# Windowed attention with sinks and a rational feed-forward layer: one sum of the gate made by an adding transfer in SBUF, all window masks on VectorE, and another program order

## The chip, the cores and the metric

The kernel runs on one core of one Trainium2 chip. A core has TensorE (matmuls, called PE in the profile), VectorE (DVE), ScalarE (ACT), GpSimd (POOL) and SyncE (SP), a memory on the core (SBUF), accumulators that matmuls write (PSUM), and 16 DMA engines that all queues share. The metric is the device time of one execution in microseconds, as the median of several. Lower is better.

## What is computed

The reference, cut to what matters:

```python
# q, k, v: (4 batches, 8 heads, 768 positions, 64), float32
scores = (1 / 8) * q @ k.T
keep = (pos_k < 4) | ((pos_q - pos_k >= 0) & (pos_q - pos_k < 128))
a = softmax(where(keep, scores, -1e9))
x = (a @ v) laid out as (3072 tokens, 512)
h = x @ w_in                                  # (3072, 2048)
P = a0 + a1*h + a2*h*h + a3*h*h*h
Q = 1 + |b0|*|h| + |b1|*h*h
out = (P / (Q + 1e-6)) @ w_out                # (3072, 512)
```

Each query sees 4 sink positions and a window of 128. Behind the attention comes a layer whose gate is a rational function, P/Q, of every element of h.

## The kernel before

**Steps.** The 3072 tokens are cut into 12 steps of 256 tokens, three to a batch. Every step goes through the same pieces: load q, k and v (POOL queue, which casts from float32 to bf16 on the way), turn k and q so that the head dimension lies on the partitions (by TensorE in the first steps, by transposing DMAs of the SP queue later), scores of each of the four head pairs (L466), exponentials (ACT, L489), the window mask, the attention product (L518), its normalisation (DVE, L542), the turned x (L568 to L598), the product with `w_in` in four slices (`gemm1`, L605), the gate, and the product with `w_out` in two halves for each of two rows of 128 tokens (`gemm2`, L669).

**The gate.** For one step h is a tile of 128 x 4096 in bf16. The gate takes it through these steps, in one piece for steps 1 to 10, in three for step 0 and in four for step 11 (`cuts`, L935):

- `copy_in` (ACT, L614): h out of PSUM, in four slices.
- `square` (L620): half of it on ACT, half on DVE; `SQ_ACT` (L120) can name another number of quarters for ACT by step.
- `magnitude` and `denominator` (DVE, L628, L634): |h| + h squared, after a scaling of x that makes the coefficients 1.
- `log_den` and `recip_den` (ACT, L653, L657): 1/Q as exp(-ln Q).
- `even` (DVE, L637): a0 + a2 h², into the tile `num`.
- `odd` and `odd_h` (DVE, L643, L647): (a1 + a3 h²) h, in place in the tile `sq`.
- `numerator` (DVE, L650): `num` + `sq`.
- `gate` (DVE, L661): `num` times 1/Q, into the tile `g`, which `gemm2` reads.

There are two buffers each of `hb`, `sq`, `den` and `g`, and one of `num`. So `even` of a step waits for `gate` of the step before, and `gate` waits for `gemm2` of two steps before.

**The masks.** Scores are computed in blocks of 64 keys by 192 queries, whose two outer thirds are cut by the triangles of the window. In the steps that `PE_MASK` (L119) names, TensorE adds a large negative number to the forbidden places by further matmuls into the same PSUM (L479 to L486). In the others DVE multiplies the exponentials with a tile of ones and zeros, `edge` (L498), one instruction for two head pairs.

**The order.** Nothing is scheduled at build time. Each piece of work has a number in the table `work` (from L697 on); the list `ORDER` (L18) is the order in which the pieces are issued, and with it the order of every engine's instructions. A negative entry is so many matmuls on a dummy tile (`spin`, L437). The figures in `piece(...)` (length, rank, load) do not act at run time. Semaphores between engines follow from the tiles. An engine runs its instructions in the order given, so a waiting instruction holds up whatever stands behind it on its engine. A transfer issued from POOL waits in the same way: for the data it reads, and for the transfer eight before it, whose semaphore it takes over.

Of the kernel before, what the change touches and what calls it, by code (L numbers as in the profile page):

```python
# [9 lines left out]
FP32 = mybir.dt.float32  # L10
BF16 = mybir.dt.bfloat16
# [7 lines left out]
    0, 2, 163, 164, 162, 154, 165, 167, 3, 166, 152, 11, 8, 151, 5, 10, 153, 12, 14, 13, 6, 15, 9,  # L19
    21, 143, 174, 1, 169, 190, -47, 191, 155, 199, 202, 196, 179, -30, 197, 172, 194, 170, 208, 195,  # L20
    160, 201, 161, 209, 157, 171, 206, 4, 7, 20, 22, 17, 145, 26, 25, 16, 24, 18, 19, 23, 192, 207,
    210, -13, 193, 200, 204, 180, 156, 212, 198, 214, 173, 181, 211, 213, 203, 205, 216, 250, 252,
    -15, 243, 217, 251, 244, -7, 218, 270, 246, 253, 219, 245, 178, 158, 271, 255, 262, 248, 247,
    249, 215, 260, 276, 159, 263, 168, 177, 261, 254, 258, 277, 256, 259, 257, 264, 278, 267, 279,
    268, 272, 265, 266, 274, 273, 220, 275, 221, 269, 579, 280, 296, 577, 281, 580, 149, 147, 184,
    30, 36, 27, 37, 38, 297, 596, 595, 282, 283, 302, 286, 583, 578, 597, 175, 586, 598, 287, 284,
    585, 587, 285, 590, 600, 601, 581, 288, 599, 584, 303, 289, 582, 317, 290, 306, 291, 293, 298,
    222, 307, 304, 292, 299, 223, 294, 323, 295, 35, 33, 32, 148, 34, 31, 39, 29, 28, 144, 47, 46,
    182, 146, 43, 48, 51, 50, 49, 185, 40, 42, 41, 150, 188, 45, 187, 186, 44, 183, 189, 224, 588,
    225, 305, 591, 602, 605, 603, 606, 604, 607, 176, 324, 592, 309, 629, 630, 625, 300, 352, 351,  # L30
    226, 314, 608, 627, 301, 626, 227, 589, 628, 308, 610, 593, 315, 312, 611, 313, 594, 609, 612,
    623, 310, 320, 332, 228, 229, 353, 624, 333, 321, 615, 311, 613, 345, 318, 319, 330, 322, 654,
    331, 632, 328, 329, 655, 652, 334, 325, 653, 335, 326, 337, 633, 614, 631, 634, 637, 327, 638,
    639, 650, 616, 342, 635, 617, 651, 316, 656, 343, 336, 354, 340, 341, 619, 338, 348, 363, 640,
    620, 339, 657, 636, 364, 346, 349, 347, 350, 361, 59, 52, 58, 61, 54, 53, 60, 62, 63, 380, 71,
    64, 57, 73, 56, 72, 55, 379, 230, 381, 355, 362, 659, 677, 359, 683, 360, 357, 678, 681, 621,
    356, 358, 682, 684, 344, 622, 618, 66, 69, 68, 67, 65, 70, 407, 74, 75, 85, 660, 641, 658, 366,
    661, 382, 365, 664, 642, 367, 679, 389, 687, 368, 665, 369, 643, 370, 666, 662, 390, 680, 385,
    371, 372, 386, 644, 374, 408, 376, 409, 77, 83, 76, 97, 373, 391, 375, 377, 392, 646, 663, 378,
    387, 647, 708, 383, 706, 388, 384, 709, 686, 648, 707, 667, 685, 394, 410, 393, 668, 395, 704,  # L40
    396, 688, 397, 710, 398, 691, 399, 669, 400, 692, 693, 401, 79, 231, 87, 84, 82, 86, 96, 233,
    81, 78, 80, 645, 437, 232, 418, 649, 402, 404, 436, 465, 464, 234, 235, 438, 466, 705, 689, 670,
    419, 711, 671, 420, 411, 673, 421, 416, 713, 412, 417, 403, 405, 406, 735, 414, 736, 415, 690,
    714, 694, 413, 712, 422, 423, 439, 428, 429, 731, 426, 715, 427, 467, 732, 695, 674, 737, 424,
    442, 733, 675, 716, 443, 700, 718, 425, 719, 430, 448, 701, 734, 738, 449, 720, 440, 446, 109,
    493, 676, 433, 702, 447, 441, 740, 696, 444, 431, 94, 89, 90, 108, 93, 92, 95, 98, 107, 100, 88,
    102, 91, 99, 110, 103, 236, 672, 703, 492, 494, 445, 432, 434, 435, 762, 763, 741, 739, 451,
    721, 456, 764, 450, 457, 717, 742, 454, 455, 758, 474, 452, 461, 697, 765, 759, 475, 121, 105,
    101, 106, 111, 104, 239, 113, 118, 115, 119, 112, 114, 120, 117, 116, 470, 722, 453, 745, 495,
    746, 768, 747, 698, 471, 743, 458, 760, 723, 472, 724, 468, 473, 761, 476, 459, 699, 237, 238,  # L50
    522, 521, 477, 767, 766, 478, 479, 469, 460, 462, 463, 789, 785, 725, 523, 744, 790, 482, 769,
    483, 727, 480, 505, 728, 506, 786, 503, 729, 504, 770, 748, 481, 749, 484, 485, 772, 524, 773,
    508, 791, 750, 501, 496, 787, 497, 792, 502, 788, 498, 513, 487, 726, 499, 486, 500, 751, 774,
    514, 507, 793, 795, 511, 512, 133, 126, 122, 489, 240, 131, 124, 123, 241, 127, 134, 550, 242,
    488, 490, 491, 816, 509, 533, 771, 775, 510, 817, 752, 534, 794, 818, 531, 532, 814, 529, 525,
    754, 819, 815, 530, 776, 796, 132, 128, 125, 135, 130, 137, 142, 139, 136, 140, 138, 141, 129,
    526, 797, 812, 799, 536, 800, 822, 516, 518, 730, 549, 755, 756, 813, 757, 753, 517, 519, 527,
    528, 520, 839, 541, 551, 801, 552, 542, 535, 820, 802, 777, 843, 537, 778, 561, 840, 798, 821,
    538, 803, 539, 515, 845, 540, 844, 562, 559, 779, 846, 560, 826, 823, 841, 842, 849, 827, 564,
    828, 847, 553, 557, 780, 546, 544, 545, 547, 781, 554, 558, 824, 548, 555, 782, 783, 556, 866,  # L60
    569, 804, 868, 848, 867, 825, 543, 563, 570, 805, 829, 850, 565, 566, 806, 869, 870, 808, 567,
    830, 853, 568, 809, 872, 854, 807, 784, 572, 574, 573, 575, 871, 851, 810, 811, 873, 875, 852,
    855, 831, 876, 874, 856, 877, 857, 576, 832, 895, 893, 833, 896, 894, 878, 835, 899, 836, 897,
    837, 900, 879, 858, 859, 834, 860, 838, 861, 862, 863, 880, 881, 901, 882, 911, 883, 931, 884,
    902, 898, 912, 922, 903, 916, 906, 913, 907, 921, 864, 885, 886, 904, 932, 914, 865, 887, 889,
    908, 923, 933, 926, 917, 909, 927, 905, 910, 947, 890, 941, 918, 928, 919, 936, 915, 934, 924,
    920, 925, 935, 891, 929, 937, 930, 938, 939, 948, 942, 949, 943, 571, 940, 950, 944, 951, 945,
    946, 892, 888, 952
# [4 lines left out]
def kernel(  # L73
# [45 lines left out]
    PE_MASK = (0, 1, 2, 3, 6, 9)  # L119
    SQ_ACT = {}  # L120
# [62 lines left out]


    k_bf, v_bd, q_bf = {}, {}, {}

    stage_a = m_sb.tile([P, MW], BF16, tag="sq", name="stage_a").bitcast(FP32)
    raw_k = stage_a[:, 0:NTS * H * D]
    stage_b = m_sb.tile([P, MW], BF16, tag="num", name="stage_b", bufs=1).bitcast(FP32)
    raw_q = stage_b[:, 0:NQ0 * H * D]  # L190
    stage_s = const_pool.tile([NS * H, D], FP32, name="stage_s")
    early = m_sb.tile([P, MW], BF16, tag="g", name="early").rearrange("p (t c) -> p t c", c=H * D)
    early_k = early[:, 0:NTS, :]
    early_q = early[:, NTS:NTS + NQ0, :]

# [868 lines left out]
```

The softmax here doesn't subtract the row's maximum and nothing guards it: scores larger than these inputs give would overflow.

## Time and profile before

| | |
|---|---|
| median of 5 runs | 255.29 us (254.15 to 257.38) |
| the profiled execution | 255.35 us, of which the profile's span is 253.6 us |
| mean granted TensorE clock | 0.993 of full speed |
| TensorE, busy | 238.2 us, 94% of the span |
| DVE, busy | 227.2 us, 90% |
| ACT, busy | 223.5 us, 88% |
| POOL, busy (issuing transfers) | 119.8 us, 47% |
| DMA moved | 27.11 MB, 107 GB/s on average |
| transfers of the POOL queue | 75568 packets, 13.00 MB |

1.75 us of the profiled execution lie outside the span. Times inside the profile count from the span's start. A row of a group gives line, engine, operation, output and inputs, the shapes and the count, then the sum of busy time, the mean of one instruction, and the idle time of the engine before them. Instructions of an engine overlap at their ends by some 0.08 us, so the distance from start to start is a little shorter than the mean: 2.20 us for a DVE operation on 128 x 4096 in bf16, whose mean is 2.28 us.

### The profile page before, as it was taken

The page shows a single profiled execution, that of the slowest core. Times are in us where ns is not written, and L with a number is a line of the kernel's source. Part 1 is how long each engine was busy: PE and PEld are TensorE (multiplying, and loading weights), DVE is VectorE, ACT ScalarE, POOL GpSimd, SP SyncE. Part 2 cuts the span into 40 slices and gives each one's busy share as a digit, 9 for nine tenths or more (in the row PEclk, how much of TensorE's full clock was granted, in tenths as well). Part 3 has the DMA queues.
Part 4 walks back from the last instruction along what each step waited for, and adds up shares of the span by engine and source line. Part 5 has one row for each costly group of instructions (what it writes and reads, how often), then busy time and mean ns, then how long its engine had stood idle before and what let it go on. Part 6 is the DMA issues. An engine that isn't in the chain of part 4 may idle for free.

```text
span 253.6 us, 5192 instructions
## 1 busy us (share of the span) xinstructions
PE 238.2 (94%) x2100; PEld 177.3 (70%) x2100; DVE 227.2 (90%) x294; ACT 223.5 (88%) x209; POOL 119.8 (47%) x170
## 2 busy tenths in 40 slices
PE   8585999999999999999999999999999999998894
PEld 7584898879667769687587676786776775763341
DVE  5238299999999999999999999999999999999991
ACT  6464699989999988989998999999999998999970
POOL 7987869698995266099905609840000000000000
PEclk9889999999999999999999999999999999999999
DMA  5999999999999989999995959994205023111103
GB/s 140 156 141 154 169 135 157 179 117 137 89 139 133 97 88 184 133 124 141 134 141 64 153 58 120 138 77 106 84 0 85 0 85 83 41 44 41 41 26 141
DMA packets 107056, 27.11 MB, mean 107 GB/s; under 512 B 97816, under 2 KB 103960, under 8 KB 107032
## 3 DMA queue, kind: packets, MB, share of 16 engines
q0 software_dynamic: 75568, 13.00, 71.2%
q1 hardware_dynamic: 29936, 12.72, 26.1%
q10 hardware_dynamic: 1528, 1.06, 1.5%
q8 instruction: 16, 0.26, 0.5%
q14 instruction: 8, 0.07, 0.1%
HBM read 27.30 MB, written 6.29 MB: 132 GB/s over the span
## 4 chain that ended last, share of the span: by engine, by line
PE 54%; DVE 25%; ACT 10%; DMA 6%; issue 3%
PE ps_out L678 21%; PE ps_h L610 19%; PE ps_o L538 6%; DVE num L651 3%; PE ps_s L476 3%; DMA stage_b<-in_q_dram 3%; DVE sq L648 2%; DVE num L640 2%; DVE kT L427 2%; ACT hb L617 2%; DVE x_n L562 2%; DVE sq L644 2%; DVE g L664 2%; DMA stage_s<-in_v_dram 2%; DVE den L635 2%
## 5 line engine op out<-in xcount | busy, mean ns | idle before, releaser
L610 PE MATMUL ps_h<-xblk,w_in_sb 128*128 128x256 bf16 x768 | 91.2, 273 | 0.3
L678 PE MATMUL ps_out<-w_out_sb,g 128*128 128x512 bf16 x368 | 86.4, 379 | 2.1 <-ACT o_t L687 2.1
L610 PEld LDWEIGHTS <-w_in_sb 128*128 128x128 bf16 x768 | 74.1, 98 | 11.2 <-issue 0.8
L241 POOL DMA_DIRECT2D v_bd<-in_v_dram x96 | 65.8, 704 | 28.0 <-PE ps_o L538 21.7
L678 PEld LDWEIGHTS <-g 128*128 128x128 bf16 x384 | 37.0, 98 | 40.2 <-issue 2.9
L617 ACT ACTIVATE hb<-ps_h 128x1024 bf16<-128x1024 f32 x48 | 48.8, 1036 | 4.8 <-PE ps_h L610 4.1
L654 ACT ACTIVATE lnq<-den,one_eps,qsc 128x4096 f32<-128x4096 bf16 (+2 forms) x17 | 47.5, 2803 | 0.5 <-DVE den L635 0.5
L494 ACT ACTIVATE e<-ps_s 128x768 bf16<-128x768 f32 x48 | 39.4, 822 | 6.8 <-PE ps_s L484 3.5
L659 ACT ACTIVATE den<-lnq 128x4096 bf16<-128x4096 f32 (+2 forms) x17 | 44.4, 2624 | 0.1
L538 PE MATMUL ps_o<-v_bd,e 128*128 128x130 bf16 x352 | 28.8, 220 | 3.8 <-DVE x_n L562 1.3
L538 PEld LDWEIGHTS <-e 128*128 128x128 bf16 x352 | 23.9, 97 | 8.4 <-DVE x_n L562 3.3
L233 POOL DMA_DIRECT2D k_bf<-in_k_dram x22 | 22.0, 1002 | 14.7 <-DMA kT_flat<-k_bf 12.1
L635 DVE TENSOR_TENSOR den<-den,sq 128x4096 bf16<-128x4096 bf16 (+2 forms) x17 | 28.1, 1658 | 0.7 <-ACT sq L624 0.5
L664 DVE TENSOR_TENSOR g<-num,den 128x4096 bf16<-128x4096 bf16 (+2 forms) x17 | 28.2, 1658 | 0.5 <-ACT den L659 0.3
L648 DVE TENSOR_TENSOR sq<-sq,hb 128x4096 bf16<-128x4096 bf16 (+2 forms) x17 | 28.1, 1659 | 0.1
L651 DVE TENSOR_TENSOR num<-num,sq 128x4096 bf16<-128x4096 bf16 (+2 forms) x17 | 28.1, 1656 | 0.0
L476 PE MATMUL ps_s<-qT,kT 128*128 128x192 bf16 x192 | 26.3, 246 | 0.5 <-ACT e L494 0.5
L624 ACT ACTIVATE sq<-hb 128x2048 bf16<-128x2048 bf16 (+1 forms) x15 | 24.3, 1630 | 0.0
L225 POOL DMA_DIRECT2D q_bf<-in_q_dram x21 | 19.1, 914 | 4.8 <-DMA w_out_sb<-in_moe_w_out_dram 2.0
L476 PEld LDWEIGHTS <-kT 128*128 128x128 bf16 x192 | 16.7, 98 | 4.7 <-issue 1.0
L562 DVE SCALAR_TENSOR_TENSOR x_n<-ps_o,ratio,rec 128x384 bf16<-128x384 f32 (+1 forms) x33 | 18.9, 573 | 1.2
L644 DVE TENSOR_SCALAR sq<-sq,acoef 128x4096 bf16<-128x4096 bf16 (+2 forms) x17 | 18.5, 1088 | 0.1
(88 smaller groups left out, 240.7 us busy)
## 6 DMA issues: line engine op xcount, KB each, us to landing
out_dram<-o_t SPq DMA_DIRECT2D x22, 256.0 KB, 2.5
v_bd<-in_v_dram POOLq DMA_DIRECT2D x96, 32.0 KB, 4.8
k_bf<-in_k_dram POOLq DMA_DIRECT2D x22, 128.0 KB, 5.4
q_bf<-in_q_dram POOLq DMA_DIRECT2D x21, 128.0 KB, 5.4
w_in_sb<-in_moe_w_in_dram POOLq DMA_DIRECT2D x4, 512.0 KB, 7.5
w_out_sb<-in_moe_w_out_dram POOLq DMA_DIRECT2D x4, 512.0 KB, 7.0
stage_b<-in_q_dram ACTq DMA_DIRECT2D x2, 384.0 KB, 7.3
stage_a<-in_k_dram SPq DMA_DIRECT2D x2, 256.0 KB, 4.2
```

Source lines behind the costliest of these rows:

```text
L241: nc.gpsimd.dma_start(out=v_bd[s][e * 64:(e + 1) * 64, i, :, e, 0:D], in_=v[b, h, g * TS:(g + 1) * TS, :].rearrange("(j p) d -> p j d", p=64))
L476: nc.tensor.matmul(half[:, n, :], lhsT=kT_fix[s % 2][:, i * NHF + 2 * a_ + n, :], rhs=qT_fix[b % 2][:, i, c:c + 192], start=not (on_pe and ...
L494: nc.scalar.activation(out=data.rearrange("p (a n) c -> p a n c", a=2), in_=ps[:, :, 0:384].rearrange("p a (n c) -> p a n c", n=2), func=A ...
L538: nc.tensor.matmul(ps_o[:, u, :], lhsT=l_, rhs=r_.rearrange("p e c -> p (e c)"), start=(m == 0), stop=(m == len(terms) - 1))
L610: nc.tensor.matmul(ps[:, n, :], lhsT=w_in_all[:, c, fc * P:(fc + 1) * P], rhs=xblk[m][:, c, :], start=(c == 0), stop=(c == NDMC - 1))
L617: nc.scalar.activation(out=hb[m][:, j * GW:(j + 1) * GW], in_=ps_h.pop((m, j)).rearrange("p n c -> p (n c)"), func=AF.Copy)
L635: nc.vector.tensor_tensor(out=den[m][:, c], in0=den[m][:, c], in1=sq[m][:, c], op=ALU.add)
L651: nc.vector.tensor_tensor(out=num[m][:, c], in0=num[m][:, c], in1=sq[m][:, c], op=ALU.add)
L654: nc.scalar.activation(out=lnq_fix[:, c], in_=den[m][:, c], func=AF.Ln, scale=qsc, bias=one_eps)
L659: nc.scalar.activation(out=den[m][:, c], in_=lnq_fix[:, c], func=AF.Exp, scale=-1.0)
L664: nc.vector.tensor_tensor(out=g_of[m][:, c], in0=num[m][:, c], in1=den[m][:, c], op=ALU.mult)
L678: nc.tensor.matmul(ps_out[m, tt], lhsT=g_of[m][:, co:co + P], rhs=w_out_all[:, fc, :], start=(fc == 0), stop=(fc == NFFC - 1))
```

## The change

- `numerator` of steps 5 to 10 is no longer a DVE instruction but one transfer of the POOL queue that adds the tile `sq` into the tile `num`, both in SBUF, 128 partitions by two pieces of 4096 bytes. Steps 0 to 4 and 11 keep the DVE instruction.
- `PE_MASK` is empty: the masks of steps 0, 1, 2, 3, 6 and 9 go from TensorE to DVE, two instructions for each step.
- `SQ_ACT` gives ACT one quarter of the squares of steps 5 to 10 in place of two; DVE takes three.
- `gate` writes into `num` in place; `num` takes the tile name `g` with three buffers, and the old `num` and `g` are gone. `even` of a step waits for `gemm2` of three steps before.
- `ORDER` is a different list, in which the pieces of all engines stand differently and 52 dummy matmuls stand in place of 112.

```diff
@@ the order @@
 ORDER = [
-    0, 2, 163, 164, 162, 154, 165, 167, 3, 166, 152, 11, 8, 151, 5, 10, 153, 12, 14, 13, 6, 15, 9,
...
+    0, 2, 163, 162, 164, 154, 3, 155, 179, 180, 156, 167, 196, 1, 165, 153, 6, 160, 173, 172, 158,
...
 ]
@@ constants @@
-    PE_MASK = (0, 1, 2, 3, 6, 9)
-    SQ_ACT = {}
+    PE_MASK = ()
+    SQ_ACT = {m: 1 for m in range(5, 11)}
+    NUM_DMA = (5, 6, 7, 8, 9, 10)
@@ the early tiles @@
-    stage_b = m_sb.tile([P, MW], BF16, tag="num", name="stage_b", bufs=1).bitcast(FP32)
+    stage_b = m_sb.tile([P, MW], BF16, tag="g", name="stage_b", bufs=3).bitcast(FP32)
...
-    early = m_sb.tile([P, MW], BF16, tag="g", name="early").rearrange("p (t c) -> p t c", c=H * D)
+    early = m_sb.tile([P, MW], BF16, tag="g", name="early", bufs=3).rearrange("p (t c) -> p t c", c=H * D)
@@ even @@
-            num[m] = m_sb.tile([P, MW], BF16, tag="num", name="num", bufs=1)
+            num[m] = m_sb.tile([P, MW], BF16, tag="g", name="num", bufs=3)
@@ numerator @@
     def numerator(m, c):
+        if m in NUM_DMA:
+            nc.gpsimd.dma_start(out=num[m][:, c], in_=sq[m][:, c], accum_op=ALU.add,
+                                max_dma_last_dim=4096)
+            return
         nc.vector.tensor_tensor(out=num[m][:, c], in0=num[m][:, c], in1=sq[m][:, c], op=ALU.add)
@@ gate @@
-        if m not in g_of:
-            g_of[m] = m_sb.tile([P, MW], BF16, tag="g", name="g")
-        nc.vector.tensor_tensor(out=g_of[m][:, c], in0=num[m][:, c], in1=den[m][:, c], op=ALU.mult)
+        nc.vector.tensor_tensor(out=num[m][:, c], in0=num[m][:, c], in1=den[m][:, c], op=ALU.mult)
@@ project_out @@
-            nc.tensor.matmul(ps_out[m, tt], lhsT=g_of[m][:, co:co + P], rhs=w_out_all[:, fc, :],
+            nc.tensor.matmul(ps_out[m, tt], lhsT=num[m][:, co:co + P], rhs=w_out_all[:, fc, :],
@@ the pieces @@
-                  sqs + [("scalars",)]
-                  + (every("gate", m - 1) or [("cast_q0", 0), ("cast_q0", 1)]))
+                  sqs + [("scalars",)] + every("even", m - 1)
+                  + ([("gemm2", m - 3, tt, 1) for tt in range(NTS)] if m >= 3 else
...
+            if m in NUM_DMA:
+                piece(("num", m, p_), "POOL", 1.0, r_ + d_ + 3.2,
+                      lambda m=m, c=c: numerator(m, c), [("odd_h", m, p_)], kind="sw", load=3.0)
```

## The prediction

> **What bounds the kernel now.** I read busy time and its slices first, then stretches of 10 us, then the chain of work that ended last, then the groups that the change touches.
>
> ```profile
> PE 238.2 (94%) x2100; PEld 177.3 (70%) x2100; DVE 227.2 (90%) x294; ACT 223.5 (88%) x209; POOL 119.8 (47%) x170
> ...
> PEclk9889999999999999999999999999999999999999
> DMA  5999999999999989999995959994205023111103
> ```
>
> Three engines are near full, the clock is granted, and the DMA engines are full up to about 170 us.
>
> ```profile
> 10.00:20.00 10.00, 8.87 (x98) 8.38 (x98) 4.14 (x18) 6.97 (x15) 7.96 (x12) 0.83 1.59 137
> ...
> 100.00:110.00 10.00, 10.00 (x88) 6.91 (x86) 9.89 (x10) 9.42 (x7) 2.30 (x4) 1.00 1.19 131
> ...
> 230.00:240.00 10.00, 7.94 (x36) 3.40 (x35) 9.99 (x16) 9.37 (x11) 0.00 (x0) 1.00 0.14 52
> ```
>
> The columns are stretch, its length, then busy PE, PEld, DVE, ACT, POOL. DVE idles at the start (18.2 us before 40, summed over four such rows) and hardly after; PE's idle time in the middle is tenths of a microsecond. So the start counts, then DVE and PE bind each other. The chain shows where each leads:
>
> ```profile
> 153.83 2.20 DVE g L664
> ...
> 226.65 3.47 PE ps_out L678 x16
> 230.14 0.60 ACT o_t L687
> ```
>
> From 137 to 187 us the chain lies on DVE (sums, gates), from 187 on PE; at the tail PE waits three times 0.69 us for ACT to empty its one output bank.
>
> ```profile
> L651 DVE TENSOR_TENSOR num<-num,sq 128x4096 bf16<-128x4096 bf16 x10 | 22.8, 2282 | 0.0
> ...
> L626 DVE TENSOR_TENSOR sq<-hb 128x2048 bf16<-128x2048 bf16 x11 | 13.4, 1216 | 0.0
> ...
> L484 PE MATMUL ps_s<-nege,ident 128*128 128x256 bf16 x32 | 8.7, 273 | 0.0
> L501 DVE TENSOR_TENSOR e<-e,edge 128x1024 bf16<-128x1024 bf16 x12 | 8.1, 684 | 0.0
> ...
> L484 PE MATMUL ps_s<-nege,ident 128*128 128x128 bf16 x32 | 4.4, 219 | 0.0
> ```
>
> These rows price the removed sums, the moved squares and both kinds of mask (busy us, mean ns, idle before). For the transfers the page gives issues, size and the median time to landing:
>
> ```profile
> v_bd<-in_v_dram POOLq DMA_DIRECT2D x96, 32.0 KB, 4.8
> ...
> w_in_sb<-in_moe_w_in_dram POOLq DMA_DIRECT2D x4, 512.0 KB, 7.5
> ```
>
> **The change, part by part.** I use distances from start to start, 0.08 us under the means: DVE 2.20 for 4096 columns, 1.14 for 2048, 0.60 for a mask; on PE, whose matmuls overlap, 0.11 for a 256-wide mask matmul and 0.055 for a 128-wide one.
>
> *Work.* DVE loses 6 numerators, 6 x 2.20 = 13.2; it gains 12 masks, 12 x 0.60 = 7.2, and 1024 more square columns in six steps, 6 x 0.53 = 3.2 (1.14 for 2048 less 0.60 for 1024). Net -2.8. PE loses 32 x 0.11 + 32 x 0.055 = 5.3. ACT loses 6 x 0.9 = 5.2 of squares (L624: 1918 ns against 1052), worth nothing while DVE and PE end last. The 60 dummy matmuls lie in waits of the start: nothing; were PE slower without them, the 0.83 of 10 to 20 us is the scale, 17% of the 8.9 us of matmuls there, 1.5 us. The in-place gate costs what the old one does, and `even` now waits for `gemm2` of three steps before, which both orders finish earlier.
>
> *Where it falls.* 8 of the 12 masks come in steps 0 to 3, while no numerator leaves before step 5. I added the start-to-start times along each engine's new and old order. From the first DVE square of step 0 to the end of the gate of step 6, DVE has 134.5 us of work before and 142.1 after: +4.8 for eight masks more, +1.6 for three larger squares, -4.4 for two numerators, and +5.9 because one set of denominator (2.20), even and odd (1.27 each) and k spreading (1.15) of a later step stands ahead of that gate; small pieces -0.3. From the first `gemm2` of step 6 to the end, PE has 66.5 before and 69.1 after. So PE waits longer for the gates and then runs without slack.
>
> *The sum.* Before: that first square starts at 32.6, the gate of step 10 comes after 195.4 us of listed work and ends in the trace at 233.2, so real time is (233.2 - 32.6) / 195.4 = 1.027 of the list; for the gate of step 6 it is 139.6 / 134.5 = 1.038. After the gate of step 10, PE has 13.8 of work and 2.9 of waits: 249.9, the last matmul. After: gate of step 6, 142.1 x 1.035 = 147.1, plus 69.1, plus 1 of waits (two output banks of step 11 now stand between those of step 10, which hides most of the 0.69s) = 217.2. By the last normalisation of step 11: 176.4 x 1.03 = 181.7, plus 4.4 for its transposing transfer (1.2 issue, 3.2 landing), plus 31.2 of PE, plus 0.7 = 218.0. I take 217.5 against 217.3 before: along this path nothing is gained.
>
> *The start.* Before, the first `gemm1` starts at 28.2 and the first square 4.4 later; in the new order a score and an exponential no longer stand between them, 1.75 + 1.0 + 0.1 = 2.9. The first `gemm1` needs the second slice of `w_in`. Adding POOL's rows in the new order (v 0.65, k and q 0.91, weights 0.8, constants 1.1, identity 0.5, `edge` 1.2) it is issued at 19.5 instead of 16.6 and lands 6.6 to 8.4 later: 26.1 to 27.9. The other arm, q, exponentials, masks and attention of step 0, I add to 25 (the stall of 4.3 us on the sink rows of v goes, since their load stands earlier; one load of q stands 6 us later; two masks add 1.2). So 27.1, first square 30.0, and -2.6 in all. The bounds of this are -4.5 and +1.
>
> *The adding transfer.* No row shows one. DVE does 12.2, 13.3, 13.0, 14.5, 13.4 and 9.0 us of listed work between `odd_h` and the gate of steps 5 to 10; that is the cover. Its issue on POOL lies between a v row (0.65) and a k row at its longest (1.6). Its time to landing is at least 2.0, the quickest 256 KB store; at most, by the `w_in` row, 1.5 MB moved in 7.5 us and here 3 MB (two reads, one write): 15. I take 8, nearest to `w_in`, as a software transfer of 1 MB read; with the issue 9, under every cover but the last, which it meets, and that gate has 3 us of slack against the gate of step 6 (its listed work plus PE's remainder is 207.9 against 211.2). So nothing, in my value; both ends stay for the range.
>
> By the Trainium skill, "Collectives: The Full Stack", section on the bandwidth ceiling, an add in the DMA path costs two source reads, so it runs at half a copy's rate; with the fit 2.0 us + bytes / 436e3 in "DMA: Bandwidth & Descriptors", section on the anatomy of one DMA, that is an estimate of 2.0 + 4.8 = 6.8, hidden too; no run here shows it.
>
> POOL issued v loads beside a DVE that was 98% busy in 0.61 to 1.45 us, median 0.65: at worst 0.8 more. The rule against the change is in "SBUF — State Buffer", section on two separate sides: a two-port DVE operation locks GpSimd out of writing descriptors, and a transfer of 620 ns took 3100; that would add 2.5 us to each issue and leave it, at 11.5, inside all covers but the last. The row is nearer.
>
> *Behind the add on POOL* stand eight loads of v for step 9 and two of k; they wait for `odd_h` of step 5, at 30.0 + 110.0 x 1.038 = 144. Their issue takes 8 x 0.65 + 2 x 0.91 = 7, and landing 4.8: 156, against a first use 129.8 us of PE's list after the first `gemm1`, with some 3 of waits 160. If the add's own transfer delays them by 8 on the same queue it is 164.
>
> **The rivals.**
>
> *1. The adding transfer is longer than its cover: slower.* Issue and landing above 13 us stall DVE at each gate. At 16 the waits are 3.8, 2.7, 3.0, 1.5, 2.6 and 7.0, in all 20.6, of which some 3 find slack: +17, 268. Decides at 13. For it: adding to a busy destination, and a queue full until 170 us. Against: after 170 the DMA is nearly free.
>
> *2. The loads behind the add come late.* PE waits 4 us at step 9 and again at step 10: up to +6 after my -2.6, 256 to 259. For it: POOL already waited 21.7 us for PE before v loads, so these are issued just in time. Against: 4 us of margin.
>
> *3. The work removed counts in full: faster.* PE's list from the first `gemm1` is 213.8 before and 209.1 after, DVE's from the first square 210.0 and 204.5. If the two don't wait for each other more than now, -4.7 to -5.5, and with the earlier start some 249.5. Against: the +7.6 at the gate of step 6.
>
> *4. It doesn't do what it says:* the add could go out in small pieces, as v does (256 bytes read at a time), and take the 15 us of the bound; it is written as two rows of 4 KB per partition, so I give this 0.02, priced with rival 1 at its 15: some +11, 263.
>
> **How the numbers follow.** The sum gives 255.35 - 2.6 = 252.8 for an execution like the profiled one, whose time is 0.06 above the median: 253. Own range of this case 250.5 to 256. Chances: this case 0.45, rival 1 (with 4) 0.33, rival 2 0.12, rival 3 0.10. Changes within 1% (252.7 to 257.8) can't be told from none. My case lies on that edge: 0.20 faster, 0.25 same. Rival 3 adds 0.10 faster, rival 2 0.05 same and 0.07 slower, rival 1 0.03 same and 0.30 slower. Together 0.30 faster, 0.33 same, 0.37 slower. The range 249.5 to 267 leaves out the best of rival 3 and the worst of rival 1.
>
> **What would show it.** Start: first `gemm1` near 27. The add: a row of 1 MB landings; under 12 us, no DVE wait before a gate; above 13, gates waiting for a DMA. Loads: PE waiting for v tiles at steps 9 and 10. Order: PE idle before `gemm2` of steps 4 to 6, a few us, and none in the last 70. Wrong I am if DVE idles after 50 us, or if PE's waits before those gates don't appear.

## The result, and the profile after

The changed kernel takes 255.53 us (median of 53 runs, 253.93 to 259.67) against 254.68 us for the kernel before (95 runs, 252.15 to 259.21): a ratio of 1.0039, 95% interval 1.0024 to 1.0054. It is 0.4% slower: the interval tells that from no change, though it lies within the 1% that the prediction took as no change. It is 2.5 us above the forecast of 253. The profiled execution took 256.53 us, its span 254.8 us; the difference of 1.7 us is as before.

The page of the changed kernel, first busy time, then the DMA engines in slices, then a queue (packets, MB, share of 16 engines) and transfers (KB each, median us to landing):

```profile
PE 231.4 (91%) x1976; PEld 170.9 (67%) x1976; DVE 224.1 (88%) x300; ACT 218.4 (86%) x209; POOL 129.3 (51%) x176
...
DMA  4999999999999949999996549989799928565113
...
q0 software_dynamic: 77200, 19.29, 94.9%
...
num<-sq POOLq DMA_DIRECT2D x6, 1024.0 KB, 9.3
...
v_bd<-in_v_dram POOLq DMA_DIRECT2D x96, 32.0 KB, 5.5
```

DVE has 3.1 us less to do than before (2.8 forecast), and PE 6.8 less (5.3 of masks, and the dummies). The six adds move 6.29 MB more through POOL's queue, and the DMA engines now stay busy to 200 us, where they were nearly free from 170 on. The same stretches as before (length, then busy PE, PEld, DVE, ACT, POOL, then granted clock):

```profile
10.00:20.00 10.00, 6.67 (x47) 6.21 (x46) 4.05 (x14) 3.93 (x8) 9.88 (x17) 0.84 1.59 150
...
230.00:240.00 10.00, 10.00 (x56) 5.31 (x55) 8.10 (x12) 9.63 (x10) 0.00 (x0) 1.00 0.33 101
```

Two things moved. At the end PE has no idle time between 230 and 240, where it had 2.1 us. At the start everything is later: PE's first matmul starts at 8.49 (1.06 before, a dummy), the first `gemm1` at 33.72 (28.20), the first DVE square at 36.72 (32.56). From that square to the end of the last matmul (251.09) it is 214.4 us, against 217.3 before. So the change is the sum of a start that is 4.2 us later in this execution and of a path behind it that is 2.9 us shorter. PE's start in the timeline (start, duration, instruction, count, and in brackets the idle time before it and what ended it):

```profile
8.49 1.01 PE L354 MATMUL ps_k<-ident,early 128*128 128x128 bf16 x4 [8.49 <-POOL ident masks.py:199]
...
14.34 0.50 PE L477 MATMUL ps_s<-qT,kT 128*128 128x192 bf16 x4 [1.21 <-ACT kT L383]
16.96 0.80 PE L440 MATMUL ps_s<-warm 128*128 128x128 bf16 x6 [2.11 <-ACT e L495]
17.55 1.49 PE L363 MATMUL ps_q<-ident,early 128*128 128x128 bf16 x6
...
33.72 3.66 PE L611 MATMUL ps_h<-xblk,w_in_sb 128*128 128x256 bf16 x32
```

DVE's first square in the same execution:

```profile
36.72 0.69 DVE L627 TENSOR_TENSOR sq<-hb 128x1024 bf16<-128x1024 bf16 x1 [2.09 <-ACT hb L618]
```

ACT's timeline, where the second load of q is issued (ACTq) and cast:

```profile
7.94 0.84 ACT L221 ACTIVATE early<-stage_b 128x768 bf16<-128x768 f32 x1 [1.54 <-DMA stage_b<-in_q_dram]
7.94 0.38 ACTq L209 DMA_DIRECT2D stage_b<-in_q_dram  x1
...
13.90 0.65 ACT L383 ACTIVATE kT<-ps_k 64x256 bf16<-64x256 f32 x2 [3.22 <-DVE kT L385]
14.56 0.84 ACT L221 ACTIVATE early<-stage_b 128x768 bf16<-128x768 f32 x1
```

The second load of q stands behind the cast of the first half, which waits for its own load: issued at 7.94, where the kernel before issued it by 3.6. It has landed by 12.0, but its cast comes at 14.56 (11.23 before), behind two spreads of k (the row at 13.90), and the matmuls that turn it at 17.55, behind six dummy matmuls that wait 2.11 us for the one bank of the scores.

The chain that ended last runs on DVE to 214 us and then on PE:

```profile
210.26 2.20 DVE num L667
212.46 1.67 DVE sq L627
214.91 4.79 DMA xblk<-x_n
219.75 1.92 PE ps_h L611 x16
...
246.77 2.59 PE ps_out L681 x12
```

Theory A: the time is the sum of the start and of a path of its own length behind it; the start costs more than the path saves, above all since the second half of q comes late. Rival B: the loads, or other transfers, set the time behind the start, so the start does not matter. Rival C: the adding transfer buys little. Theory G: the add's transfer lengthens the last transposing transfer (4.79 us in this chain, 3.2 in the median before), and that costs the end.

### The profile page after: what moved, and what is told of

It reads as the page before. It is cut to its first block, busy times and chain, and to the rows that moved or that the text cites. A ratio compares the mean times of both kernels' runs of the same rounds, so it can differ in the third digit from the quotient of the medians.

```text
span 254.8 us, 4991 instructions
## 1 busy us (share of the span) xinstructions
PE 231.4 (91%) x1976; PEld 170.9 (67%) x1976; DVE 224.1 (88%) x300; ACT 218.4 (86%) x209; POOL 129.3 (51%) x176
## 3 DMA queue, kind: packets, MB, share of 16 engines
q10 hardware_dynamic: 1528, 1.06, 1.4%
HBM read 27.30 MB, written 6.29 MB: 132 GB/s over the span
## 4 chain that ended last, share of the span: by engine, by line
DVE 54%; PE 29%; issue 6%; DMA 4%; ACT 3%; POOL 2%; SPq 0%; ACTq 0%
PE ps_out L681 12%; PE ps_h L611 8%; DVE den L636 7%; DVE sq L649 7%; DVE num L667 6%; DVE sq L627 5%; DVE x_n L563 4%; DMA xblk<-x_n 4%; DVE num L641 4%; DVE sq L645 4%; DVE e L502 3%; DVE kT L428 3%; DVE num L656 3%; PE ps_o L539 2%; DVE den L632 2%
## 5 line engine op out<-in xcount | busy, mean ns | idle before, releaser
L681 PE MATMUL ps_out<-w_out_sb,num 128*128 128x512 bf16 x368 | 86.1, 379 | 1.4 <-ACT o_t L690 0.7
L242 POOL DMA_DIRECT2D v_bd<-in_v_dram x96 | 69.1, 815 | 16.1 <-DMA num<-sq 6.8
L681 PEld LDWEIGHTS <-num 128*128 128x128 bf16 x384 | 36.8, 98 | 39.3 <-DVE num L667 1.3
L653 POOL DMA_DIRECT2D num<-sq x6 | 7.3, 1214 | 59.9 <-ACT lnq L659 18.7
L667 DVE TENSOR_TENSOR num<-num,den 128x4096 bf16<-128x4096 bf16 (+2 forms) x17 | 28.1, 1657 | 2.0 <-ACT den L664 1.9
L649 DVE TENSOR_TENSOR sq<-sq,hb 128x4096 bf16<-128x4096 bf16 (+2 forms) x17 | 28.2, 1659 | 0.2
L226 POOL DMA_DIRECT2D q_bf<-in_q_dram x21 | 20.8, 999 | 14.7 <-DMA qT<-q_bf 13.8
L477 PE MATMUL ps_s<-qT,kT 128*128 128x192 bf16 x192 | 24.6, 254 | 1.9 <-ACT kT L383 1.2
L477 PEld LDWEIGHTS <-kT 128*128 128x128 bf16 x192 | 17.5, 102 | 5.9 <-ACT kT L383 1.5
L641 DVE TENSOR_SCALAR num<-sq,acoef 128x4096 bf16<-128x4096 bf16 (+2 forms) x17 | 18.4, 1081 | 2.0 <-ACT sq L625 2.0
L625 ACT ACTIVATE sq<-hb 128x1024 bf16<-128x1024 bf16 (+1 forms) x15 | 19.3, 1284 | 0.1
```

Of the source, the lines that this page charges most:

```text
L242: nc.gpsimd.dma_start(out=v_bd[s][e * 64:(e + 1) * 64, i, :, e, 0:D], in_=v[b, h, g * TS:(g + 1) * TS, :].rearrange("(j p) d -> p j d", p=64))
L477: nc.tensor.matmul(half[:, n, :], lhsT=kT_fix[s % 2][:, i * NHF + 2 * a_ + n, :], rhs=qT_fix[b % 2][:, i, c:c + 192], start=not (on_pe and ...
L649: nc.vector.tensor_tensor(out=sq[m][:, c], in0=sq[m][:, c], in1=hb[m][:, c], op=ALU.mult)
L667: nc.vector.tensor_tensor(out=num[m][:, c], in0=num[m][:, c], in1=den[m][:, c], op=ALU.mult)
L681: nc.tensor.matmul(ps_out[m, tt], lhsT=num[m][:, co:co + P], rhs=w_out_all[:, fc, :], start=(fc == 0), stop=(fc == NFFC - 1))
```

## The experiments

Sixteen runs, all against the kernel before. Profiled executions differ from each other by a microsecond or so, most of it in the start: the six profiles with the changed kernel's unaltered start (of the changed kernel, num_dve, masks_pe and add_twice, and two of num9_dve) show the first square at 34.1 to 36.7, mean 35.4. In the table, "path" is from the first square to the end of the last matmul in the profiled execution; times are medians. Each ratio is to the kernel before as it was measured beside that kernel, with medians of 254.5 to 255.3, so two kernels are better compared by their ratios than by their medians.

| kernel | first `gemm1` | first square | path | time | ratio (95%) |
|---|---|---|---|---|---|
| before | 28.2 | 32.6 | 217.3 | 254.68 | |
| changed | 33.7 | 36.7 | 214.4 | 255.53 | 1.0039 (1.0024 to 1.0054) |
| start_late | 35.6 | 38.7 | 215.8 | 259.42 | 1.0177 (1.0132 to 1.0222) |
| q0_early | 31.5 | 34.5 | 215.3 | 255.33 | 1.0022 (0.9995 to 1.0050) |
| ident_early | 32.7 | 35.8 | 215.8 | 255.54 | 1.0056 (1.0013 to 1.0098) |
| q0_path | 29.1 | 32.1 | 214.9 | 253.99 | 0.9989 (0.9956 to 1.0022) |
| start_fix | 29.0 | 32.0 | 216.7 | 252.80 | 0.9926 (0.9889 to 0.9963) |
| start_fix_spins | 28.5 | 31.5 | 214.9 | 252.70 | 0.9943 (0.9914 to 0.9972) |
| start_fix_store | 29.2 | 32.2 | 215.0 | 253.10 | 0.9966 (0.9936 to 0.9997) |
| best_try | 29.4 | 33.6 | 214.6 | 252.82 | 0.9938 (0.9904 to 0.9971) |
| best_win | 29.7 | 33.2 | 214.4 | 254.20 | 0.9956 (0.9921 to 0.9992) |
| start_before | 30.0 | 33.1 | 218.1 | 258.90 | 1.0141 (1.0092 to 1.0191) |
| num_dve | 32.8 | 35.9 | 223.0 | 264.78 | 1.0385 (1.0339 to 1.0431) |
| masks_pe | 32.2 | 35.2 | 215.3 | 255.73 | 1.0014 (0.9987 to 1.0040) |
| num9_dve | 31.7 | 34.7 | 215.5 | 258.02 | 1.0118 (1.0062 to 1.0173) |
| add_twice | 31.1 | 34.1 | | 290.45 | 1.1408 (1.1354 to 1.1461) |

### What the adding transfer buys: num_dve, add_twice, num9_dve

```diff
-    NUM_DMA = (5, 6, 7, 8, 9, 10)
+    NUM_DMA = ()
```

> The changed kernel's order, with the sum of the numerator of steps 5 to 10 as a tensor_tensor on DVE again, at the place in DVE's order where the transfer stands in POOL's. Theory A (DVE ends last between the first square and step 6, and the transfer takes 2.2 us a step off it unseen): DVE 13.2 us busier, time 261 to 268. Rival C (PE is the bound behind step 6, so DVE has room for the sums, and the transfer buys little): 254 to 258.

264.78 us, 9.3 more than the changed kernel. Stretches of this kernel (same columns):

```profile
170.00:180.00 10.00, 8.59 (x75) 5.82 (x75) 9.80 (x15) 7.11 (x5) 0.00 (x0) 1.00 0.09 21
...
190.00:200.00 10.00, 8.23 (x80) 6.42 (x80) 9.89 (x12) 7.77 (x7) 0.00 (x0) 1.00 0.25 25
```

DVE is full and PE idles 1.4 and 1.8 us of ten, where in the changed kernel both are full. Along DVE's order the same instructions come 1.3 us earlier than in the changed kernel at 149 and 10.8 later at 223. So of the 13.2 us that the transfers take off DVE, about 9 lie on the path (8.6 between first square and last matmul). Rival C falls.

```diff
             nc.gpsimd.dma_start(out=num[m][:, c], in_=sq[m][:, c], accum_op=ALU.add, ...)
+            nc.gpsimd.dma_start(out=num[m][:, c], in_=sq[m][:, c], accum_op=ALU.add, ...)
```

> The changed kernel with each of the six adding transfers issued twice, one behind the other, so that the odd half of the numerator counts twice in steps 5 to 10. With the measured 9.3 us to landing the pair takes 1.2 + 2 x 9 = 19 to 20 us. Theory A (the cover is what I listed, 12.2, 13.3, 13.0, 14.5, 13.4 and 9.0 us): DVE waits some 7 us at five gates and 10 at the last, 35 to 45 us in all, time 285 to 300. Rival (the list understates the cover, the gates could be later without anyone waiting): under 275. Rival (the second one overlaps with the first): landing under 14 us and time under 262.

290.45 us, 34.9 more, just under what the listed covers gave (35 to 45). Waits in this kernel (in all, how often, longest):

```profile
POOL num L655 <- DMA num<-sq: 48.9, 6, 10.0
DVE num L669 <- DMA num<-sq: 26.1, 5, 9.2
```

The second add is issued only when the first has landed (POOL waits 8 us each time), so a pair takes about 20 us, and now gates wait for it, five times, up to 9.2 us. That wait of POOL is for the first add's semaphore, so the program sets the order; whether two such transfers would overlap without it is not shown. In the changed kernel no gate does: DVE's waits there are 1.9 us in all, for ACT. The single add is hidden, though at step 5 only just: it lands at 159.36 and the gate starts at 159.96; at the other five steps 2.3 to 5.4 us are left. The cover that I added up from DVE's list is of the right size.

```diff
-    NUM_DMA = (5, 6, 7, 8, 9, 10)
+    NUM_DMA = (5, 6, 7, 8, 10)
 DVE: norm.11.0
+DVE: num.9
```

> The changed kernel with the sum of step 9 alone on DVE again, placed in DVE's order behind the last normalisation of step 11; the other five sums stay transfers. Theory G (in the changed kernel the add of step 9, issued at 210.2 and moving until about 220, lengthens the last transposing transfer of x, which starts at 214.9, and PE runs without a gap from its landing to the end): the transfer lands in 2.5 to 3.3 us instead of 4.8, PE's first gemm1 of step 11 and the last matmul come 1.5 to 2.3 us earlier, time 253.2 to 254.2. Rival (the 2.2 us more on DVE behind that normalisation come out at the end, or the transposing transfer is slow for another reason): 255.3 or more.

Theory G is right about the transfer and wrong about the time: without the add of step 9 the last transposing transfer lands in 2.5 us, but the time is 258.02, not 253.2 to 254.2. PE's waits in the changed kernel from 200 us on:

```profile
PE ps_out L681 <- ACT o_t L690: 0.7, 1, 0.7
PE ps_h L611 <- DMA xblk<-x_n: 0.2, 1, 0.2
```

The transfer stands in the chain with 4.79 us, but while it moves PE works at `gemm2` of step 8, to 219.5; PE waits 0.2 us for it. The chain names what came last, not what it cost. In num9_dve PE runs straight from that `gemm2` into step 11, and its path (215.5) is no shorter than the others. This holds for the changed kernel; start_before, below, does wait for this transfer.

### The masks: masks_pe

```diff
-    PE_MASK = ()
+    PE_MASK = (2, 3, 6, 9)
```

> The changed kernel's order, with the masks of steps 2, 3, 6 and 9 on PE again: 8 masks of 0.60 us less on DVE, and 0.165 x 16 x 4 / 3 = 3.5 us more on PE (a third of the sum of 5.3 us for each two steps). Theory A (DVE ends last before step 6, PE behind): the relief before and the load behind cancel, 254.5 to 256.5. Rival D (the masks' place is what the gain behind the start comes from, PE being the bound all through): 257 to 260. Rival E (the masks on DVE cost their whole 4.8 us): 251 to 253.

255.73: PE has 44 matmuls more and DVE 3.4 us less to do, and the time is 0.2 us off the changed kernel's (by the ratios 0.6 us shorter, inside the interval). Relief before and load behind cancel; rivals D and E fall.

### Whether the start counts: start_late, start_before

```diff
-  12 dummy matmuls before scores.1.3
+  72 dummy matmuls before scores.1.3
```

> The changed kernel with 60 more dummy matmuls on PE shortly before the first gemm1 (60 x 0.055 = 3.3 us). Theory A (what stands behind the start has a length of its own, so a start that is later by some us ends later by as much): first square 3 to 3.5 us later, time 258 to 259.5. Rival B (the loads on POOL's queue, or the transfers, set the time behind the start): time 255.3 to 256.8, the delay being taken up between 40 and 170 us.

259.42 us, 3.9 more (3.5 by the ratios), with a first square 3.3 us later than the mean of the six. Path 215.8: what is put in front comes out at the end. Rival B falls in this direction.

```diff
-  the changed order up to the first gemm1
+  the order of the kernel before up to there, masks of step 0 on DVE
```

> The changed kernel whose program order up to the first gemm1 is that of the kernel before (with its 60 dummy matmuls more, its early identity matrix, its early second q load), the two masks of step 0 staying on DVE; from there the changed kernel's order. Theory A (the change is a late start of some +4 to +5 us and a gain of some 3 us behind it): first gemm1 at 28 to 29.5, first square on DVE at 31 to 33, from there to the last matmul 214 to 216 as in the changed kernel, time 250 to 252. Rival B (what stands behind the start is bound by something that does not move with it, the loads on POOL's queue): the start comes earlier by as much, but the time stays at 254 to 256, with PE or DVE waiting for a DMA between 60 and 160 us.

258.90 us: a miss. The first square is 3.7 us earlier than in the changed kernel's profile, as Theory A expects, but the path is 218.1. The same DVE instructions are 2.75 us early at 42, 2.3 at 127, 1.75 at 184 and none at 227. PE's waits behind 36 us:

```profile
PE ps_h L611 <- DMA xblk<-x_n: 2.6, 2, 1.8
PE ps_out L681 <- ACT o_t L690: 1.9, 2, 1.2
```

against 1.3 and 0.7 in the changed kernel: transposing transfers and stores that land late. The longest of these waits, 1.8 us at 219.8, is for the transfer of Theory G, which takes 6.4 us here beside the add of step 9 (4.8 in the changed kernel, 2.5 without that add). So an early start can be given back in part. That the adds are to blame for a part of it is argued, since no run without them has this start. And five of the six executions took 258.6 to 259.9, while the profiled one took 256.6; num9_dve shows the same (255.65 profiled, median 258.0). I profiled both once more:

> The same kernel as start_before, profiled once more. Theory I (most of its executions lose 2 to 3 us in one place): DVE or PE shows one wait or a stretch of the granted clock of that size that the first profile lacks, time 258 to 260. Rival: as the first profile, 256 to 257, and its place stays open.

> The same kernel as num9_dve, profiled once more. Theory I: one wait or stretch of the granted clock of 2 to 3 us that the first profile lacks, time 257 to 259. Rival: as the first profile, 255 to 256.5, and its place stays open.

256.55 and 256.75 us, with the first profiles' picture (path 217.9 and 215.6; in start_before the same transfer takes 6.5 us and PE waits 1.9 for it). Theory I got no support: what the slower executions do is not in any trace I have, and stays open.

### Which part of the start: q0_early, ident_early, q0_path, start_fix

```diff
 ACT:  load_q0.1
+ACT:  load_q0.0
 ACT:  load_a, clear_vs, load_vs, babs, clear_v.2, cast_q0.1
-ACT:  load_q0.0
```

> The changed kernel with one move: the second load of q of step 0 is issued on ACT's queue right behind the first, not behind the first cast. Theory A1 (this load is the largest part of the late start): the cast of the second half starts near 9 to 11 instead of 14.6, the first gemm1 at 31 to 32.5 instead of 33.9, time 253 to 254.5. Rival A2 (the identity matrix, or the waits for the one bank of the scores, hold step 0): first gemm1 within 0.7 of 33.9, time 255 to 256.

255.33 us, 0.2 less than the changed kernel, though the first `gemm1` is 2.2 us earlier than in the changed kernel's profile; against the mean of the six profiles with that start (32.4) it is 0.8. The start is as Theory A1 said and the time as Rival A2 said. ACT's row shows why so little comes of it: the load is issued by 2.3, and the cast still stands behind the spreads of k:

```profile
13.66 0.84 ACT L221 ACTIVATE early<-stage_b 128x768 bf16<-128x768 f32 x1
```

So it is the place of the cast and of the matmuls behind it that holds the second half of q, not the load alone.

```diff
 POOL: sink_consts
+POOL: ident
 POOL: load_v.0.2, ..., load_q.3
-POOL: ident
```

> The changed kernel with one move: the identity matrix is made right behind POOL's first constants, before the first load of v, not behind six loads. Theory A3 (it holds the first transposing matmuls to 8.5 us, and the first half of step 0 behind them): those start near 6.6, but the second half waits for the second load of q as before, so the first gemm1 comes at most 1 us earlier; time 254.8 to 255.6. Rival (it is the largest of the four moves): first gemm1 2 us or more earlier and time under 254.3.

255.54: nothing. PE's longest wait of the start, 8.5 us for the identity matrix, cost nothing, since the second half of q came later still.

```diff
 ACT:  load_q0.1
+ACT:  load_q0.0
 ACT:  ..., cast_q0.1
-ACT:  load_q0.0
 ACT:  clear_v.1, clear_kT.1
+ACT:  cast_q0.0
 ACT:  spread_k0.2.1, spread_k0.3.1
-ACT:  cast_q0.0
 PE:   turn_k0.0, turn_q0.1, turn_k0.1
+PE:   turn_q0.0
 PE:   14 dummies, scores.0.2, 6 dummies
-PE:   turn_q0.0
```

> Three of the four moves in the start: the second load of q, its cast and its transposing matmuls; the identity matrix stays behind the six loads. Theory A5 (the chain of the second half of q is the whole of it; the identity matrix is hidden): first gemm1 at 28.5 to 30, time 252.5 to 253.3, as with all four. Rival (the identity matrix at 8.4 becomes what ends last once q is early): first gemm1 at 30 or later, time 253.8 or more.

> The changed kernel with four moves in the start and nothing else: the identity matrix right behind POOL's first constants, the second load of q right behind the first on ACT's queue, its cast behind the clearing of kT, and its transposing matmuls behind those of k. Theory A: first square near 31 to 33 us, time 251.5 to 253.5. Rival B (an earlier start is given back behind it, as when the whole start of the kernel before was put in): first square as early, time 255 to 258.

q0_path is this edit, start_fix has the move of the identity matrix too. PE's start in start_fix:

```profile
6.62 1.03 PE L354 MATMUL ps_k<-ident,early 128*128 128x128 bf16 x4 [6.62 <-DVE early L215]
...
11.20 1.46 PE L363 MATMUL ps_q<-ident,early 128*128 128x128 bf16 x6 [0.32 <-ACT early L221]
...
29.04 3.66 PE L611 MATMUL ps_h<-xblk,w_in_sb 128*128 128x256 bf16 x32
```

The second half of q is turned at 11.2 instead of 17.55, and the first `gemm1` starts at 29.04, in q0_path at 29.06. start_fix takes 252.80 us, 1.1% less than the changed kernel and 0.7% less than the kernel before: a version that beats both. q0_path's trace shows the same start, its median, 253.99, is 1.2 us higher and above the 252.5 to 253.3 expected. The two traces can't tell why: q0_path's is of its fastest execution (252.42) and start_fix's of one of its slowest (254.23). So that the three moves of q bring the early start is shown; how much of the time is theirs, and whether the identity matrix has a part, stays open.

### What the start is worth beyond that: start_fix_spins, start_fix_store, best_try, best_win

```diff
+PE:   47 dummies
 PE:   turn_k0.0
+PE:   13 dummies
 PE:   turn_q0.1
```

> The kernel with the four moves of the start, and the 60 dummy matmuls that the change took out, 47 before the first transposing matmuls and 13 behind them, in time in which PE waits. Theory A4 (the dummy matmuls in waits cost and bring nothing): within 0.7 us of the four moves alone, 252.1 to 253.5, first gemm1 within 0.7 of 29.0. Rival W (without them the clock is granted lower around 15 to 25 us, where the profiles of the changed order show 0.50 to 0.84 in most executions and 1.00 in some): the granted clock stays at 1.00 in that stretch and the time is 1 us or more shorter, under 251.8. Rival W2 (the other way: more work early brings the lower clock): a dip in the clock, 253.5 or more.

252.70, as without them. PE's start in this kernel:

```profile
8.19 0.83 PE L363 MATMUL ps_q<-ident,early 128*128 128x128 bf16 x6 [0.70 <-ACT early L221]
...
11.45 0.99 PE L440 MATMUL ps_s<-warm 128*128 128x128 bf16 x14
...
18.21 1.01 PE L440 MATMUL ps_s<-warm 128*128 128x128 bf16 x8 [1.06 <-ACT e L495]
```

The added dummies do make PE faster early: the six matmuls that turn q take 0.83 us, against 1.46 in start_fix. The 14 dummies behind them take 0.99 us against 1.78 in the changed kernel and in start_fix, though in q0_early, without added dummies, they took 0.99 too. But PE is slow again later, at 18.2 (8 in 1.01, against 0.61 in start_fix), after three waits of about 1 us each; the first `gemm1` gains 0.5 us, the time nothing.

```diff
+SP:   store.4.1
 SP:   turn_x.9.0
-SP:   store.4.1
```

> The kernel with the four moves of the start, and one move more: the second store of step 4 stands before the first transposing transfer of x of step 9 on SP's queue, not behind it. Theory H (that store, ready at 162.9, was issued only at 172.4 since SP stood waiting for x, landed beside the add's transfer at 177.5, and so held an output buffer, ACT for 1.8 us and PE for 1.9): no wait of ACT for a store near 176, last matmul 1 to 1.8 us earlier, time 251 to 252. Rival (DVE sets the time there, and PE catches up later): within 0.5 us of the four moves alone, 252.3 to 253.3.

What the edit removes, in ACT's timeline of start_fix:

```profile
177.54 0.60 ACT L690 ACTIVATE o_t<-ps_out 128x512 f32<-128x512 f32 x1 [1.76 <-DMA out_dram<-o_t]
```

That wait is gone from the trace, and the profiled execution's path is 1.7 us shorter (215.0 against 216.7). The median, 253.10, is not lower than start_fix's. Theory H holds for the wait, not for the time.

```diff
 (start_fix_store, and)
+ACT:  place_q0.0 before spread_k0.2.1, place_q0.1 behind exps.0.2
+ACT:  placed_x.0.1 before exps.1.2
+PE:   scores.0.0 before turn_q.4
-PE:   6 dummies before scores.0.3, 8 before sink_scores.0
```

> The four moves of the start, the store of step 4 as above, and three moves more in the start: the first half of q is placed as soon as it is transposed, its scores stand before the transposing matmuls of a later q, and two groups of dummy matmuls (6 and 8) that waited for the one bank of the scores are left out. Theory A: first gemm1 at 27 to 28, time 249.5 to 251.3. Rival B (an earlier start is given back behind it): 252 or more.

252.82, as Rival B, not the 249.5 to 251.3 of Theory A. The scores come 2 to 3 us earlier, and then PE waits in front of the first `gemm1`:

```profile
PE ps_h L611 <- DMA w_in_sb<-in_moe_w_in_dram: 2.8, 1, 2.8
```

Behind that wait PE is slow: the 32 matmuls of the first `gemm1` take 5.33 us, against 3.66 in start_fix, so the first square is later than there.

```diff
 (best_try, and)
+POOL: load_w_in.1
 POOL: load_w_in.0, edges, load_v.1.3, load_v.1.2, load_k.2.1, load_k.2.0
-POOL: load_w_in.1
```

> The kernel before it (seven moves in the start and at the store of step 4), with the second slice of the first weights, which the first gemm1 needs, loaded before the first slice instead of five issues later. There PE waited 2.8 us for that slice, until 29.4. Theory A (the start's length comes out one to one, and that slice was what ended last): first gemm1 at 26.3 to 27.5, first square 29 to 30.5, time 250 to 251.5. Rival B: first gemm1 as early, time 252 or more.

254.20, a miss. The weights are there in time, and PE waits 2.4 us for k of step 2, which its loads now bring later; the first `gemm1` starts at 29.69. In these two orders the loads are the bound near 29 us: one load earlier makes another one late.

## Why the prediction was wrong, step by step

**The start: the step that failed.** "The other arm, q, exponentials, masks and attention of step 0, I add to 25", and so "27.1, first square 30.0, and -2.6 in all". Measured: first `gemm1` at 31.1 to 33.7 and first square at 34.1 to 36.7 in six profiles, +2.8 in the mean (against the one profile of the kernel before). I counted the late load of q as one load six us later, without following who waits for it: its cast stands on ACT's queue behind two spreads of k that wait for DVE (13.90), the matmuls that turn it stand on PE behind dummies that wait for an exponential, and the scores of step 0 go through one bank one after the other, 2.6 to 3.6 us apart. With the load early and the cast in its old place the cast still starts at 13.66 (q0_early); three moves that concern only this half of q bring the first `gemm1` to 29.06 (q0_path). The arm of the weights held in the changed kernel: I had `w_in`'s second slice landing at 26.1 to 27.9; it was issued at 19.3 (forecast 19.5) and landed at 27.0. But where q comes earlier that slice lands later, at 28.4 in q0_path, 28.7 in start_fix and 29.4 in best_try, after 8.7 to 9.6 us instead of 7.6. So no order here reached the 27.1, even with q out of the way.

**The clock without the dummies.** Taken as nothing, at worst 1.5 us. The size holds: 0.5 us at the first `gemm1`, nothing in the time. But I read the granted clock from the column alone, and that reads 1.00 between 10 and 15 us in the changed kernel, where 14 dummy matmuls took 1.78 us, at 0.127 each; the durations show the slow phase, the column doesn't. The Trainium skill, "TensorE: Matmul & The Clock Gate", part 1, has PE throttled to half its rate until it has been busy for some 3.4 us, and again after an idle window. The 1.78 against 0.99 us, a factor of 1.8, agrees with it; that a whole idle window lay before the slow matmuls at 18.2, which come with the dummies too, is not shown, as PE waited there three times for about 1 us.

**The path behind the start: 217.5 forecast, 214.4 measured** (214.4 to 216.7 over the kernels whose start alone was altered, 218.1 in start_before). This is the second term that was off, in the other direction. PE's arm was right, DVE's was not: I multiplied the list with 1.035 to the gate of step 6 and 1.03 to the last normalisation, as before. That gate ends at 180.27, 143.6 after the first square, on a list of 142.1: 1.010; the normalisation 178.2 on 176.4: 1.010. PE's rest from there, 70.8, is what I had (70.1). DVE's waits make little of this: it idled 2.7 us in that stretch before and 2.0 after. But it was busy for 136.9 us on a list of 134.5 before and for 141.5 on 142.1 after, so its work up to that gate grew by 4.6 us, not by the 7.6 that I listed. Some instructions were shorter than before (a copy into `kT` 543 ns in the mean against 637, an `odd` of 4096 columns 1347 against 1408); why stays open. So rival 3 (the removed work counts) was nearer for this term than my own case: PE's list shrank by 4.7 and the time from the first `gemm1` to the last matmul by 4.3. Masks on DVE cost what they save: with eight of them back on PE (masks_pe) the time is 0.2 us off.

**The adding transfer: right.** 8 us to landing forecast, 8.0 to 11.2 measured, median 9.3; issue 1.2; no gate waits for it, and doubled it costs 34.9. At step 10, where I listed a cover of 9.0, there were 11.8 us from the issue to the gate. Its worth (9.3 us in num_dve) was not a term of mine, as I compared whole lists. The Trainium skill's "Collectives: The Full Stack" (bandwidth ceiling), with the fit of "DMA: Bandwidth & Descriptors" (anatomy of one DMA), gave an estimate of 6.8, short by 2.5. The lock that "SBUF — State Buffer" (two separate sides) describes, 2.5 us more for an issue beside a busy DVE, shows in no issue (1.18 to 1.23); but five of the six issues ran almost wholly beside TENSOR_TENSOR instructions, so this is no test of it for DVE's other operations.

**Loads of v behind the add: no wait of PE, but not for my reason.** I forecast a landing at 156, or at 164 if the add delays them on the same queue, and a first use at 160. The add did delay them. Of the 24 loads of v of steps 9 to 11, the 18 that were issued while an add was moving took 7.6 to 10.6 us, and none landed before that add; the other six took 3.5 to 4.3. In num_dve, the same order without adds, all 24 took 2.2 to 5.3. At step 9 the add landed at 159.36 and the first load behind it at 159.97; POOL waited 4.7 us for that landing before the last three loads (the transfer eight before), and these landed by 164.6. No wait of PE names a load of v, since the first use came only at 169.6. So the delay of rival 2 happened and its price did not.

**Order.** Forecast was PE idle a few us before `gemm2` of steps 4 to 6 and none in the last 70. It idles 1.7 us between 120 and 180, 1.1 of them for a transposing transfer, and 0.9 between 210 and 220, 0.7 of them for an output buffer. PE's waits for the gates of steps 4 to 6, which the prediction made a sign of being wrong if they failed to appear, did not appear: the gates came earlier than forecast, as said of the path.

**The sum.** Start +2.8 (mean of the profiles) and path -1.9 (215.4, the mean of the changed kernel and those whose start alone was altered, start_before left out, against 217.3) make +0.9; measured is +0.85. I had -2.6 and +0.2. The start was 5.4 us worse than I said and the path gave 2.1 of them back; that the forecast is off by no more than 2.5 us is in part luck. The rival that ended slower, the add longer than its cover, was the wrong mechanism. Two of the rivals' prices did not follow from my own sum either: +17 on 252.8 makes 270, not 268, and rival 3's -4.7 makes 248, not 249.5; the result hangs on neither.

## What to carry to other kernels

In the first 30 us, where no engine is full yet, follow each load through every queue it passes, to the instruction that waits last: summing engines' work there misses waits behind waits. For the full part of the kernel, sums along DVE's order came to within 1.0% of the time in the changed kernel and 2.7 to 3.8% in the kernel before, so a scale taken from one order need not fit another. The longest wait, or the transfer that a chain names, may cost nothing in one order and something in another; ask what else the waiting engine would have done, and take the price from its idle time. An add moved from a full engine to a DMA queue pays when the engine has its landing time of other work in between, and what to check is which transfers share the queue with it: here they landed only after the add.

## What the hardware showed that I had not expected

- A transfer issued on the adds' queue while an add was moving landed only after it: 18 loads of v took 7.6 to 10.6 us, against 2.2 to 5.3 for the same loads in num_dve.
- Transposing transfers of x beside the adds land later: from 150 us on 4.2 us in the median, against 2.8 for the same ones in num_dve; the last two took 3.4 and 4.8 us, and 2.5 each in num9_dve, where the add of step 9 was taken out. For stores this is not shown: one beside an add took 5.1 us in start_fix (issued at 172.4), but three took 5.1 to 5.7 at 105 to 118 in the changed kernel, ahead of all adds.
- Between profiles of the same start the first square scatters by 2.6 us (34.1 to 36.7), which is more than most of the edits here are worth; the part of it that a trace shows is PE's slow phase, at 17 to 19 us in every one and again at 24 to 26 in the two slowest.
- Making the identity matrix took POOL 1.28 us in two of these six profiles, 0.55 in a third and 0.29 in the other three, in the same order of instructions. In the three long ones a whole cast of DVE ran in that time; a clearing on DVE beside it did not lengthen it (0.29 at 7.08 in num9_dve). That the cast is the reason is not shown.
